# Scatters of rows that no longer wait for one another, in a fused attention and mixture-of-experts kernel

## The chip, the cores and the metric

The kernel runs on one core of a Trainium2 chip. The metric is the device time of one execution in microseconds (us). The kernel before takes 4299.98 us, the median of three runs (4298.31 to 4304.7).

## The reference

Three stages run on 24576 tokens (8 batches of 3072) of width 256, all in float32.

```python
# 1 attention without softmax, gated by u
attn = np.maximum(z @ z.T / S, 0.0) ** 2          # per batch, S = 3072, z is S x 64
x = u * (attn @ v)
# 2 dense layer, d_ff = 1024
h = x @ w_in;  e = np.exp(h - h.max(-1)); solu = h * e / (e.sum(-1) + 1e-9)
x = (solu - mean) / np.sqrt(var + 1e-6) * g_ln @ w_out
# 3 one expert of eight per token
logits = x @ w_gate;  expert = argmax(logits);  gate = softmax(logits)[expert]
out[mask_e] = gate[mask_e] * (np.maximum(x[mask_e] @ w1[e], 0) @ w2[e])
```

## The kernel before, in words

Products are made at nearly float32 accuracy by splitting each operand into a high and a low part and adding three matmuls (`mm3`, lines 104 to 107).

**The main stage** walks through 48 chunks of 512 tokens. A chunk takes 24 slots, one slot for each block of 128 keys; there are 1152 slots (NS). A dictionary `events` lists what else is done in a slot: loads, and, for the chunk before, the dense layer (`blk_h` to `blk_y`) and the routing (`blk_scale`, `blk_logits`, `blk_route`, `blk_rows`). The program is written out in the order of slots, and each engine does its own instructions strictly in that order. The routing passes small tiles between GpSimd and VectorE: GpSimd computes `vv` (lines 600 to 604), VectorE needs it at line 608, and so on at lines 642 and 648 and at lines 676 and 679.

**The scatter of rows.** When the expert and the place of each token are known, `blk_scatter` (lines 684 to 691) writes 128 rows of 264 floats to a table in HBM, `sorted_rows`, by an indirect DMA that GpSimd issues. There are four per chunk, 192 in all. Rows of one expert lie together, so the table can then be read in units of one expert each.

**The expert stage** has 62 units: 37 of 512 rows whose places are fixed by an early table (made after 44 chunks are counted, by `table_step(0, ...)`), 4 of 512 rows and 21 of 256 rows from a later table. Each has 8 steps. In step k, `up(k)` makes one eighth of the hidden layer, and `downs` multiplies the eighth of two steps before (LAG = 2) by w2. Around the steps of a unit stand the loads of a later unit: its rows by `load_x` (line 843; issued by GpSimd for units 0 and 1, by SyncE for the rest), its weights by `load_w` (line 849), split into high and low parts by ScalarE and VectorE at lines 854 and 855. The last chunks' dense layer and routing run between the first steps of this stage, on the same engines.

**The scatter of outputs.** After the last step of a unit, `down` copies one or two PSUM banks of 128 x 512 to SBUF (line 926 on VectorE, line 928 on ScalarE, in turn) and right behind each copy writes two indirect DMAs to the output (line 931). There are 206 of them, all issued by GpSimd. Each row of the output is written once.

**What orders these DMAs.** Dependencies are worked out tile by tile from what an instruction reads and writes. All scatters of rows write the same table, and an indirect write may touch any row of it. So each scatter of rows waits until the scatter before it has landed, and until loads of unit rows that were issued before it have landed; and each load of unit rows waits for all scatters before it. Scatters of outputs wait for one another likewise. The wait stands on the issuing engine's queue (GpSimd, or SyncE for loads), and what is written behind it on that engine waits too.

In one slot the order is: scores, buffers taken, `up(k)`, the events of the slot, the attention products, `downs(k - LAG)`, then the elementwise work.

Of the kernel before, what the change touches and what calls it, by code (L numbers as in the profile page):

```python
# [10 lines left out]
F32 = mybir.dt.float32  # L11
# [3 lines left out]
U32 = mybir.dt.uint32  # L15
# [18 lines left out]
def attention_moe_kernel(ctx, tc, u, v, z, w_in, w_out, g_ln, w_gate, w1, w2, out):  # L34
    nc = tc.nc
    B, S, D = u.shape
# [4 lines left out]
    N = B * S  # L41
# [29 lines left out]
    n_early = max(0, -(-(SNAP * CH - NE * (FULL - 1)) // FULL))  # L71
    n_late = max(0, -(-(N - n_early * FULL - NE * (FULL - 1)) // FULL))
    n_half = (N - (n_early + n_late) * FULL + NE * (HALF - 1)) // HALF
    units = [FULL] * (n_early + n_late) + [HALF] * n_half
    NU = len(units)
# [4 lines left out]
    const = ctx.enter_context(tc.tile_pool(name="const", bufs=1))  # L80
# [13 lines left out]
    tail_i = const.tile([1, NE], I32, name="tail_i")  # L94
    n_used = const.tile([1, NE + 1], F32, name="n_used")
    index = const.tile([1, n_most], F32, name="index")

    V, A, G, T = nc.vector, nc.scalar, nc.gpsimd, nc.tensor

# [29 lines left out]
    with ExitStack() as st:  # L129
# [4 lines left out]
        ap = st.enter_context(tc.tile_pool(name="ap", bufs=2))  # L134
# [363 lines left out]


        h_t, p_t, pt_t, y_t, st_t = {}, {}, {}, {}, {}  # L500
        pb_t, pT_t = {}, {}

        def blk_h(c, t, kd):
# [88 lines left out]
        def small(name, shape, dt=F32):  # L592
            return sp.tile(shape, dt, tag=name, name=name)
# [41 lines left out]
        def blk_route(c, part):  # L635
            s, y = st_t[c], y_t[c]
            k4 = 4 * NE
            if part == 0:
                s["m"] = small("gm", [P, 4])
                V.tensor_reduce(out=s["m"], in_=s["lg"], axis=AX.X, op=ALU.max)  # L640
            elif part == 1:
                G.tensor_tensor(out=s["lg"], in0=s["lg"], in1=s["m"].unsqueeze(2).to_broadcast([P, 4, NE]),
                                op=ALU.subtract)
            elif part == 2:
                s["ex"] = small("gx", [P, 4, NE])
                A.activation(out=s["ex"], in_=s["lg"], func=AF.Exp)
                s["key"] = small("gk", [P, 4, NE])
                V.scalar_tensor_tensor(out=s["key"], in0=s["lg"], scalar=0.0, in1=first_key,
                                       op0=ALU.is_equal, op1=ALU.mult)
            elif part == 3:  # L650
                V.tensor_reduce(out=s["m"], in_=s["key"], axis=AX.X, op=ALU.max)
                s["gs"] = small("gs", [P, 4])
                V.tensor_reduce(out=s["gs"], in_=s["ex"], axis=AX.X, op=ALU.add)
            elif part == 4:
                s["oh"] = small("oh", [P, 4, NE], BF16)
                V.tensor_tensor(out=s["oh"], in0=s["key"], in1=s["m"].unsqueeze(2).to_broadcast([P, 4, NE]),
                                op=ALU.is_equal)
                G.tensor_scalar(out=s["gs"], in0=s["gs"], scalar1=1e-9, scalar2=0.0, op0=ALU.add, op1=ALU.add)
            elif part == 5:
                oh = s["oh"]  # L660
                s["cum"] = cum = small("cum", [P, 4, NE], BF16)
                G.tensor_copy(out=cum[:, 0], in_=counts)
                for t in range(3):
                    G.tensor_tensor(out=cum[:, t + 1], in0=cum[:, t], in1=oh[:, t], op=ALU.add)
                G.tensor_tensor(out=counts, in0=cum[:, 3], in1=oh[:, 3], op=ALU.add)
                V.reciprocal(out=s["gs"], in_=s["gs"])
                G.tensor_scalar(out=y[:, :, D], in0=row_id, scalar1=float(c * CH), scalar2=0.0,
                                op0=ALU.add, op1=ALU.add)
            elif part == 6:
                s["rk"] = rk = ps_m.tile([P, CH], F32, tag="m", name="rk")  # L670
                T.matmul(out=rk[:, :k4], lhsT=upper, rhs=s["oh"].rearrange("p t e -> p (t e)"), start=True, stop=False)
                T.matmul(out=rk[:, :k4], lhsT=ones, rhs=s["cum"].rearrange("p t e -> p (t e)"), start=False, stop=True)
                s["ps"] = small("ps", [P, 4, NE])
                V.tensor_tensor(out=s["ps"], in0=rk[:, :k4].rearrange("p (t e) -> p t e", t=4), in1=e_base, op=ALU.add)
            elif part == 7:
                G.tensor_tensor(out=s["ps"], in0=s["ps"], in1=s["oh"], op=ALU.mult)
            elif part == 8:
                s["pf"] = small("pf", [P, 4])
                V.tensor_reduce(out=s["pf"], in_=s["ps"], axis=AX.X, op=ALU.add)
            else:  # L680
                s["pi"] = small("pi", [P, 4], I32)
                G.tensor_copy(out=s["pi"], in_=s["pf"])

        def blk_scatter(c, t):
            pi = st_t[c]["pi"]
            G.indirect_dma_start(  # L686
                out=xs[:DUMMY], out_offset=bass.IndirectOffsetOnAxis(ap=pi[:, t:t + 1].bitcast(U32), axis=0),
                in_=y_t[c][:, t, :], in_offset=None, bounds_check=DUMMY - 1, oob_is_err=False)
            if t == 3:
                y_t.pop(c)  # L690
                st_t.pop(c)
# [69 lines left out]
                    V.tensor_tensor(out=n_used[:, :NE], in0=n_used[:, :NE], in1=now, op=ALU.add)  # L761
                yield

        table = {}

        def table_step(key, *args):
            if key not in table:
                table[key] = unit_table(*args)
            next(table[key], None)

        def pad_tail(e):
# [8 lines left out]
        raw_w, w_set, xT_t, hT_b, o_b, xr_t, gi_t, id_t = {}, {}, {}, [], [], {}, {}, {}  # L780
# [45 lines left out]
        def dma_of(i):  # L826

            return G if i < 2 else nc.sync

        def load_x(i, part=None):  # L830

            n = units[i]
            if not part:
                x_row[i] = dma_of(i).value_load(row_i[0:1, i:i + 1], min_val=0, max_val=DUMMY - (n if n == FULL else 0))
                xr_t[i] = xrow.tile([P, KD * CH], F32, tag="x", name="x")
                gi_t[i] = sp.tile([P, FULL // P], F32, tag="gi", name="gi", bufs=6)
            xv = xr_t[i][:, :KD * n].rearrange("p (k a j) -> p k a j", k=KD, j=32)
            unit = xs[ds(x_row[i], n)]
            src = unit[:, :D].rearrange("(a i) (k b j) -> k b i a j", i=32, b=4, j=32)
            todo = [(xv[b * 32:(b + 1) * 32, k], src[k, b]) for b in range(4) for k in range(KD)]  # L840
            todo.append((gi_t[i][:, :n // P], unit[:, D:D + 1].rearrange("(q p) w -> p (q w)", p=P)))
            for dst, x in todo if part is None else todo[3 * part:3 * part + 3]:
                dma_of(i).dma_start(out=dst, in_=x)

        def load_w(i, k):
            e = dma_of(i).value_load(expert_i[0:1, i:i + 1], min_val=0, max_val=NE - 1)
# [30 lines left out]
        LAG = 2  # L877
# [3 lines left out]
        def piece(i, name, at, n):  # L881
            return w_set[i % 2, name][at // CH][:, at % CH:at % CH + n]
# [27 lines left out]
        def down(k):  # L910
            i, m = steps[k]
            hT = hT_t.pop(k)
            if m == 0:
                y_p[i] = y_banks(i)
            for r in range(units[i] // P):
                rs = slice(r * P, (r + 1) * P)
                y = y_p[i][r // 2][:, r % 2 * D:(r % 2 + 1) * D]
                mm3(y, hT[0][:, rs], hT[1][:, rs], piece(i, "w2h", m * D, D), piece(i, "w2l", m * D, D),
                    m == 0 and r % 2 == 0, m == KE - 1, skip_group_check=True)
            if m < KE - 1:  # L920
                return
            for h, y in enumerate(y_p.pop(i)):
                o_n[0] += 1
                o = o_b[o_n[0] % len(o_b)]
                if o_n[0] % 2:
                    V.tensor_copy(out=o, in_=y)
                else:
                    A.activation(out=o, in_=y, func=AF.Copy)
                for r in range(2):
                    q = 2 * h + r  # L930
                    G.indirect_dma_start(
                        out=out, out_offset=bass.IndirectOffsetOnAxis(ap=id_t[i][:, q:q + 1].bitcast(U32), axis=0),
                        in_=o[:, r * D:(r + 1) * D], in_offset=None, bounds_check=N - 1, oob_is_err=False)

        def downs(k):

# [6 lines left out]
        for c in range(NCHUNK):  # L943
# [11 lines left out]
            else:  # L955

                late = j >= NCB - 2
# [59 lines left out]
        early = [(0, n_early, FULL)], False  # L1017
        late = [(n_early, n_late, FULL), (n_early + n_late, n_half, HALF)], True
# [26 lines left out]
        for part in range(3):  # L1045
            at(s0 + XA + 3 * part, load_x, 0, part)
# [11 lines left out]
        for i in range(NU):  # L1058
            k0 = NS + i * KE
            k1 = k0 + KE  # L1060
            late = max(0, 5 - i)
# [16 lines left out]
        with tc.manual_schedule():  # L1078
            for n in range(min(lo_slot, -LA), hi_slot + 1):
                i = n + LA  # L1080
                k = n - NS
                if 0 <= i < NS and not is_kept(i):
                    pe_scores(i)
                for fn, args in events.get(n, []):
                    if fn is take:
                        fn(*args)
                if 0 <= k < NP:
                    up(k)
                for fn, args in events.pop(n, []):
# [52 lines left out]
```

## Time and profile before

| | us |
|---|---|
| median of 3 runs | 4299.98 |
| the profiled execution's own time | 4297.59 |
| its span, first to last instruction | 4296.0 |
| TensorE busy (98% of the span) | 4218.8 |
| VectorE busy (74%) | 3173.4 |
| ScalarE busy (65%) | 2773.7 |
| GpSimd busy (32%) | 1368.9 |

Mean granted TensorE clock: 0.994 of full speed. The 16 DMA engines moved 719.11 MB.

In the profile PE is TensorE's matmuls, PEld its weight loads, DVE VectorE, ACT ScalarE, POOL GpSimd, SP SyncE; a q behind a name is the engine's sequencer. `out_y L931` and the like name the tile written and the line of the kernel. An arrow in brackets names the instruction that ended an idle time; a DMA there means that its data had landed. PEclk is the mean clock granted to TensorE in a stretch: 1.00 is 2.4 GHz, 0.50 is 1.2 GHz, and values between mean that it changed within the stretch.

### The profile page before, as it was taken

The numbers are of one execution on the slowest core, as the hardware profiler recorded it, in microseconds if no ns is written. First come the engines' busy times: TensorE is split into PE (matmuls) and PEld (weight loads), VectorE is DVE, ScalarE is ACT, GpSimd is POOL, SyncE is SP. The second block draws the span as 40 slices with busy tenths as digits, with TensorE's granted clock in tenths as the row PEclk, the third lists the DMA queues.
The fourth block names the chain that finished last, engine by engine and source line by source line (L and its number), as shares of the span: only waits on it lengthen the run. The fifth ranks groups of instructions, "written<-read, shape, count | busy, mean of one in ns | idle before, by whom it ended". The sixth has DMA issues, their size and how long they took to land.

```text
span 4296.0 us, 74103 instructions
## 1 busy us (share of the span) xinstructions
PE 4218.8 (98%) x23314; PEld 3659.4 (85%) x23314; DVE 3173.4 (74%) x5485; ACT 2773.7 (65%) x5104; POOL 1368.9 (32%) x2852
## 2 busy tenths in 40 slices
PE   7999999999999999999999999999889999999998
PEld 5888888888888888888888888888788899999998
DVE  8778787777878777787877778777655555555686
ACT  7767776776777677667767766775544444444565
POOL 5135224323522432352244235224322111111111
PEclk9999999999999999999999999999999999999999
DMA  6898789789888988997898898789655555555585
GB/s 160 168 173 180 171 181 176 165 183 174 179 170 182 175 166 183 173 177 171 182 174 168 183 174 176 169 169 181 143 143 132 147 147 134 145 137 147 156 221 162
DMA packets 2444332, 719.11 MB, mean 167 GB/s; under 512 B 2251933, under 2 KB 2325917, under 8 KB 2443936
## 3 DMA queue, kind: packets, MB, share of 16 engines
q1 hardware_dynamic: 2402016, 603.29, 69.2%
q0 software_dynamic: 40864, 110.95, 8.7%
q8 instruction: 182, 2.98, 0.3%
q14 instruction: 214, 1.75, 0.1%
q10 hardware_dynamic: 1056, 0.13, 0.0%
HBM read 442.35 MB, written 273.49 MB: 167 GB/s over the span
## 4 chain that ended last, share of the span: by engine, by line
PE 81%; issue 5%; DMA 4%; DVE 2%; SPq 2%; POOL 1%; ACT 1%; POOLq 0%; DVEq 0%; ACTq 0%
PE o L105 11%; PE o L106 11%; PE o L107 11%; PE yp L105 4%; PE yp L107 4%; PE yp L106 4%; PE h L512 4%; PE h L513 4%; PE h L516 4%; PE s L444 3%; PE s L445 3%; PE y L107 3%; PE y L106 3%; PE y L105 3%; PE g L105 3%
## 5 line engine op out<-in xcount | busy, mean ns | idle before, releaser
L106 PE MATMUL o<-al,vw 128*128 128x512 f32 x2304 | 908.2, 394 | 7.8 <-DVE al L465 7.3
L105 PE MATMUL o<-ah,vw 128*128 128x512 f32 x2304 | 907.8, 394 | 1.7 <-DVE ut L489 1.7
L107 PE MATMUL o<-ah,vw 128*128 128x512 f32 x2304 | 898.7, 390 | 0.0
L450 ACT ACTIVATE r<-s 128x512 f32<-128x512 f32 x704 | 416.7, 592 | 405.6 <-PE s L445 397.1
L460 ACT ACTIVATE ah<-a 128x512 fp32r<-128x512 f32 x832 | 525.3, 631 | 201.6 <-issue 99.5
L465 DVE TENSOR_TENSOR al<-a,ah 128x512 fp32r<-128x512 f32 x832 | 581.4, 699 | 15.7 <-ACT ah L460 14.7
L107 PEld LDWEIGHTS o<-ah,vw 128*128 128x128 f32 x2304 | 433.7, 188 | 94.4
L106 PEld LDWEIGHTS o<-al,vw 128*128 128x128 f32 x2304 | 433.6, 188 | 94.2 <-DVE al L465 16.3
L105 PEld LDWEIGHTS o<-ah,vw 128*128 128x128 f32 x2304 | 433.6, 188 | 84.9 <-ACT ah L460 2.1
L455 ACT ACTIVATE a<-r 128x512 f32<-128x512 f32 x704 | 438.0, 622 | 58.2 <-DVE al L465 29.5
L899 ACT ACTIVATE zw_x<-g 128x512 fp32r<-128x512 f32 (+1 forms) x332 | 179.9, 542 | 428.9 <-PE g L107 425.2
L107 PE MATMUL yp<-gw,ptl 128*128 128x264 f32 x1536 | 437.8, 285 | 7.0 <-DVE ptl L102 7.0
L105 PE MATMUL yp<-gw,pth 128*128 128x264 f32 x1536 | 438.8, 286 | 1.1 <-ACT pth L101 1.1
L106 PE MATMUL yp<-gw,pth 128*128 128x264 f32 x1536 | 438.0, 285 | 0.0
L900 DVE SCALAR_TENSOR_TENSOR zw_x<-g,zw_x 128x512 fp32r<-128x512 f32 (+1 forms) x332 | 205.6, 619 | 308.8 <-ACT zw_x L899 308.7
L102 DVE TENSOR_TENSOR ptl<-pT,pth 128x512 fp32r<-128x512 f32 x384 | 264.2, 688 | 215.8 <-ACT pth L101 213.7
L686 POOL DMA_INDIRECT sorted_rows<-y,pi x192 | 211.7, 1102 | 390.3 <-DMA sorted_rows<-y,pi 307.9
L513 PE MATMUL h<-w_in,xt 128*128 128x512 f32 x768 | 304.9, 397 | 0.0
L512 PE MATMUL h<-w_in,xt 128*128 128x512 f32 x768 | 304.6, 397 | 0.0
L105 PEld LDWEIGHTS yp<-gw,pth 128*128 128x128 f32 x1536 | 289.2, 188 | 16.9 <-ACT pth L101 1.5
L106 PEld LDWEIGHTS yp<-gw,pth 128*128 128x128 f32 x1536 | 289.9, 189 | 15.0
L107 PEld LDWEIGHTS yp<-gw,ptl 128*128 128x128 f32 x1536 | 290.1, 189 | 7.7 <-DVE ptl L102 7.7
(271 smaller groups left out, 10665.7 us busy)
## 6 DMA issues: line engine op xcount, KB each, us to landing
vw_x<-in_moe_w SPq DMA_DIRECT2D x120, 1024.0 KB
pT<-moved SPq DMA_DIRECT2D x768, 128.0 KB
sym<-kept SPq DMA_DIRECT2D x1520, 64.0 KB
kept<-sym SPq DMA_DIRECT2D x316, 256.0 KB
moved<-pb SPq DMA_DIRECT2D x528, 128.0 KB
moved<-pb POOLq DMA_DIRECT2D x240, 128.0 KB, 3.1
x<-sorted_rows SPq DMA_DIRECT2D x312, 64.0 KB
sym<-kept SPq DMA_DIRECT2D x68, 256.0 KB
```

The costliest lines, as they stand in the source:

```text
L102: V.tensor_tensor(out=lo, in0=src, in1=hi.bitcast(F32), op=ALU.subtract)
L105: T.matmul(out=out, lhsT=lh, rhs=rh, start=start, stop=False, **kw)
L106: T.matmul(out=out, lhsT=lh, rhs=rl, start=False, stop=False, **kw)
L107: T.matmul(out=out, lhsT=ll, rhs=rh, start=False, stop=stop, **kw)
L450: A.activation(out=r, in_=s_t.pop(n), func=AF.Relu)
L455: A.activation(out=a, in_=r_t.pop(n), func=AF.Square)
L460: A.activation(out=h, in_=a_t[n], func=AF.Copy)
L465: V.tensor_tensor(out=l, in0=a_t[n], in1=ah_t[n].bitcast(F32), op=ALU.subtract)
L512: T.matmul(out=h[:, fs], lhsT=w[:, 0, kd, ts_], rhs=w_in_t[0][:, kd, fs], start=(kd == 0), stop=False)
L513: T.matmul(out=h[:, fs], lhsT=w[:, 0, kd, ts_], rhs=w_in_t[1][:, kd, fs], start=False, stop=False)
L686: G.indirect_dma_start(out=xs[:DUMMY], out_offset=bass.IndirectOffsetOnAxis(ap=pi[:, t:t + 1].bitcast(U32), axis=0), in_=y_t[c][:, t, :], ...
L900: V.scalar_tensor_tensor(out=lo, in0=h, scalar=0.0, in1=hi.bitcast(F32), op0=ALU.max, op1=ALU.subtract)
```

## The change

Four things are changed.

- A scatter of rows is declared independent of other scatters of rows and of the loads of the 37 early units. The loads of the early units are declared independent of scatters of chunks that the early table did not count ("late rows"). They still wait for scatters of counted chunks, and loads of later units still wait for all.
- Scatters of outputs are declared independent of one another.
- A scatter of outputs is not written behind its eviction any more, but at the start of a later step: one step later for the first bank of a unit, two steps later for the second. Those of the last unit stay where they were.
- Ahead of every scatter, and ahead of a group of row loads that GpSimd issues, GpSimd clears one float (`between`).

```diff
+        def between():
+            G.memset(gap, 0.0)
+
+        def apart(i, *groups, why):
+            for g in groups:
+                tc.declare_no_dep(i.ins, group=g, reason=why)
+
         def blk_scatter(c, t):
             pi = st_t[c]["pi"]
-            G.indirect_dma_start(
+            between()
+            i = G.indirect_dma_start(
                 out=xs[:DUMMY], out_offset=bass.IndirectOffsetOnAxis(ap=pi[:, t:t + 1].bitcast(U32), axis=0),
                 in_=y_t[c][:, t, :], in_offset=None, bounds_check=DUMMY - 1, oob_is_err=False)
+            apart(i, "rows", "late rows", why="every token has a row of its own")
+            apart(i, "early units", why="units of the early table are full of rows counted before")
+            tc.add_to_no_dep_group("late rows" if table and c not in counted else "rows", i.ins)
...
+            if dma_of(i) is G:
+                between()
             for dst, x in todo if part is None else todo[3 * part:3 * part + 3]:
-                dma_of(i).dma_start(out=dst, in_=x)
+                d = dma_of(i).dma_start(out=dst, in_=x)
+                if i < n_early:
+                    apart(d, "late rows", why="units of the early table are full of rows counted before")
+                    tc.add_to_no_dep_group("early units", d.ins)
...
                 for r in range(2):
-                    q = 2 * h + r
-                    G.indirect_dma_start(
-                        out=out, out_offset=bass.IndirectOffsetOnAxis(ap=id_t[i][:, q:q + 1].bitcast(U32), axis=0),
-                        in_=o[:, r * D:(r + 1) * D], in_offset=None, bounds_check=N - 1, oob_is_err=False)
+                    if i == NU - 1:
+                        send(i, 2 * h + r, o[:, r * D:(r + 1) * D])
+                    else:
+                        sends[k + 1 + h].append((i, 2 * h + r, o[:, r * D:(r + 1) * D]))
+
+        sends = defaultdict(list)
+
+        def send(i, q, o):
+            between()
+            d = G.indirect_dma_start(
+                out=out, out_offset=bass.IndirectOffsetOnAxis(ap=id_t[i][:, q:q + 1].bitcast(U32), axis=0),
+                in_=o, in_offset=None, bounds_check=N - 1, oob_is_err=False)
+            apart(d, "out", why="every token has a row of its own")
+            tc.add_to_no_dep_group("out", d.ins)
...
                     if fn is take:
                         fn(*args)
+                for args in sends.pop(k - LAG, []):
+                    send(*args)
                 if 0 <= k < NP:
                     up(k)
```

(`counted` holds the chunks whose routing was written before the early table is begun.)

## Rows read from the trace of the kernel before

**Rows 1.** Busy us, instructions, PEclk, DMA share and GB/s by stretch:

```profile
200.00:3000.00 2800.00, 2795.94 (x14227) 2370.94 (x14227) 2206.66 (x3779) 1995.57 (x3598) 1034.55 (x2422) 1.00 0.88 175
3000.00:3420.00 420.00, 386.57 (x2326) 345.33 (x2325) 247.16 (x461) 185.14 (x342) 111.60 (x192) 0.96 0.57 139
3420.00:4283.00 863.00, 862.71 (x5981) 806.13 (x5980) 558.21 (x995) 446.37 (x898) 154.30 (x155) 1.00 0.60 159
```

**Rows 2.** Waits of PE from 3000 to 3420: us in total, times, longest:

```profile
PE g L105 <- DVE zw_x L900: 26.3, 7, 7.1
PE yp L107 <- DVE ptl L102: 6.6, 1, 6.6
```

**Rows 3.** Timeline of PE: start, us, instruction, idle before it and its releaser:

```profile
3050.45 0.50 PE L105 MATMUL g<-vw_x 128*128 128x512 f32 x1 [0.99 <-DVE zw_x L900]
...
3359.16 0.79 PE L105 MATMUL g<-a_x,zd_x 128*128 128x512 f32 x1 [3.40 <-DVE zw_x L900]
...
3387.00 0.80 PE L105 MATMUL g<-vw_x 128*128 128x512 f32 x1 [3.57 <-DVE zw_x L900]
```

**Rows 4.** Stretches of 10 us from where PE resumes (columns of rows 1):

```profile
3016.53:3026.53 10.00, 10.00 (x45) 8.79 (x46) 6.59 (x10) 3.54 (x6) 5.95 (x19) 0.78 0.64 132
3103.01:3113.01 10.00, 10.00 (x59) 9.17 (x60) 8.66 (x16) 3.64 (x7) 5.30 (x17) 0.83 0.21 55
3137.35:3147.35 10.00, 10.00 (x54) 8.96 (x55) 8.71 (x18) 4.76 (x9) 3.26 (x10) 0.84 0.21 52
3171.27:3181.27 10.00, 10.00 (x54) 8.94 (x55) 8.96 (x15) 4.76 (x9) 3.62 (x3) 0.83 0.30 87
3230.12:3240.12 10.00, 10.00 (x44) 8.85 (x45) 4.39 (x8) 1.72 (x3) 1.94 (x8) 0.70 0.81 158
3359.16:3369.16 10.00, 10.00 (x54) 8.92 (x55) 9.64 (x33) 4.51 (x9) 2.97 (x3) 0.84 0.17 61
3387.00:3397.00 10.00, 10.00 (x48) 8.73 (x49) 8.00 (x28) 4.39 (x9) 1.94 (x2) 0.70 0.67 214
```

**Rows 5.** Waits of DVE for POOL from 3000 to 3420:

```profile
DVE yi L608 <- POOL vv L604: 24.6, 3, 9.1
...
DVE gk L648 <- POOL lg L642: 12.5, 1, 12.5
...
DVE pf L679 <- POOL ps L676: 9.2, 1, 9.2
```

**Rows 6.** Timeline of POOL around the stall that ends at 3137.35:

```profile
3118.94 1.07 POOL L931 DMA_INDIRECT out_y<-a_x,ids  x1 [9.21 <-DVE a_x L926]
...
3132.89 0.98 POOL L931 DMA_INDIRECT out_y<-a_x,ids  x1 [3.22 <-DMA out_y<-a_x,ids]
3133.88 0.26 POOL L642 TENSOR_TENSOR lg<-lg,gm 128x32 f32<-128x32 f32 x1
```

**Rows 7.** Timeline of POOL before the stall that ends at 3016.53:

```profile
3013.06 1.02 POOL L686 DMA_INDIRECT sorted_rows<-y,pi  x1 [4.64 <-DMA gi<-sorted_rows]
```

**Rows 8.** Waits of SP's queue, 3150 to 3420, and ACT's timeline at 3357:

```profile
SPq L843 <- DMA sorted_rows<-y,pi: 43.6, 4, 17.5
...
3357.15 0.63 ACT L854 ACTIVATE vw_x<-vw_x 128x512 fp32r<-128x512 f32 x1 [6.41 <-DMA vw_x<-in_moe_w]
```

**Rows 9.** Timeline of POOL, the last two scatters:

```profile
4284.25 0.97 POOL L931 DMA_INDIRECT out_y<-p_x,ids  x1 [6.84 <-DVE p_x L926]
4286.60 0.97 POOL L931 DMA_INDIRECT out_y<-p_x,ids  x1 [1.39 <-DMA out_y<-p_x,ids]
```

**Rows 10.** Line 931: ns min/median/max of scatters from `a_x`, and all landings:

```profile
L931 POOL DMA_INDIRECT out_y<-a_x,ids x108: 967/972/1608, 3087.2 to 4267.4; - x108
...
DMA to landing us min/median/max: 2.1/3.6/6.8
```

**Rows 11.** POOL's smallest clear (groups by line: busy us, mean ns of one):

```profile
L1127 POOL MEMSET const-float32-1.0<- 128x1 f32 x1 | 0.1, 99 | 0.0
```

**Rows 12.** Waits of ACT from 300 to 2950:

```profile
ACT pth L101 <- DMA pT<-moved: 30.2, 21, 4.7
```

More of the change, by code (lines that the diff above doesn't have):

```diff
@@ L96, in attention_moe_kernel @@
     index = const.tile([1, n_most], F32, name="index")
+    gap = const.tile([1, 1], F32, name="gap")
     V, A, G, T = nc.vector, nc.scalar, nc.gpsimd, nc.tensor
@@ L500, in attention_moe_kernel @@
         h_t, p_t, pt_t, y_t, st_t = {}, {}, {}, {}, {}
+        table, routed, counted = {}, [], []
         pb_t, pT_t = {}, {}
@@ L665, in blk_route @@
                 G.tensor_tensor(out=counts, in0=cum[:, 3], in1=oh[:, 3], op=ALU.add)
+                routed.append(c)
                 V.reciprocal(out=s["gs"], in_=s["gs"])
@@ L762, in unit_table @@
                 yield
-        table = {}
         def table_step(key, *args):
@@ L768, in table_step @@
                 table[key] = unit_table(*args)
+                if key == 0:
+                    counted.extend(routed)
             next(table[key], None)
```

## The prediction

> **What bounds the kernel now.** I read the busy time by stretch first, to see where TensorE (PE) is not full [rows 1]. From 200 to 3000 us it is idle for 4.06 of 2800 us, and from 3420 to 4283 for 0.29 of 863: there PE is the bound, and shorter waits on GpSimd (POOL) or SyncE (SP) buy nothing. Between them, from 3000 to 3420, it is idle for 33.4 of 420 us and its clock averages 0.96. This is where the last chunks' routing runs among the first expert units, and the only place where the change can pay much. The long waits of POOL elsewhere are no loss; a reader who adds them up over the span would expect far too much.
>
> Then PE's waits in that stretch: 6.6 us once and 26.3 us in seven pieces, all ended by VectorE (DVE) [rows 2]. In PE's timeline one of the seven is a mere 0.99 us at 3050 [rows 3]; without it seven stalls are left, together 6.6 + 26.3 - 0.99 = 31.9 us. Behind each of them the clock is low: in the 10 us after PE resumes it averages 0.70 to 0.84, so part of that time ran at 1.2 GHz and the rest at 2.4 [rows 4]. The work lost there is 10 us times one minus the clock: 2.2 + 1.7 + 1.6 + 1.7 + 3.0 + 1.6 + 3.0 = 14.8 us. The stage is full and at full speed elsewhere, so the seven stalls cost 46.7 us with their slow restarts.
>
> Last, who was late. Five stalls are DVE waiting for a small routing result of POOL: 24.6 us in three waits, 12.5 in one and 9.2 in one, 46.3 in sum [rows 5]. POOL's own timeline says why: for the stall that ends at 3137, POOL began the four scatters of a unit at 3118.94, each held until the one before had landed, and got to the routing at 3133.88, 14.9 us later, though the instruction itself takes 0.26 us [rows 6]. For the stall that ends at 3016 the scatters of rows did the same and also waited for loads of unit 0, up to 4.64 us at a time [rows 7]. DVE works in order, so the split of the next hidden layer stood behind the routing instruction that waited, and PE behind that. The other two stalls, 3.40 and 3.57 us [rows 3], come from SP: loads of unit rows waited 43.6 us in four pieces, the longest 17.5, for scatters of rows of the last chunks; the weight loads queue behind them, and ScalarE (ACT) then sat 6.41 us waiting for weights [rows 8].
>
> **The change part by part.**
>
> *Waits between scatters go.* POOL is held by a scatter only for its own instruction, 0.97 us at the median and 1.61 at most [rows 10], and the added clear, for which 0.1 us is taken from POOL's smallest one [rows 11]. Four scatters in a row so cost 4 x 1.07 = 4.3 us, at worst 4 x 1.71 = 6.8, in place of 14.9. Even if all four stood ahead of the routing, as now, the result at 3133.88 would come 8.1 to 10.6 us sooner, more than the 7.1 us that PE stalled [rows 2]. The same test for the five together: their 46.3 us of DVE waits turned into 31.9 - 3.40 - 3.57 = 24.9 us of PE stalls, so PE stands about (46.3 - 24.9) / 5 = 4.3 us of such a wait without loss. The five waits average 9.3 us. If each shrinks by the share of [rows 6], 10.6 of 14.9, 2.7 us are left of it, and by the worst share, 8.1 of 14.9, 4.2 us: both within the margin, the second barely. All five are counted as gone.
>
> *Scatters of outputs move one and two steps back.* At most two then stand in one step, ahead of that step's `up` and routing on POOL, and their data were evicted one step before, so POOL no longer sits at their head for the eviction with routing behind. What moves is 204 of 206 indirect DMAs, on POOL's queue alone; SP's and ACT's order is untouched. The SBUF buffers of the evictions stay occupied 1 to 2 steps longer, but are used again only after one unit of 8 steps (two buffers, at the start) or two (four buffers). A landing takes 6.8 us at most [rows 10], while the 8 steps of a unit of 256 rows are about 12 us long and of one of 512 rows about 22. Cost: nothing; this cover would be gone only if a scatter took a whole unit.
>
> *Loads of early units no longer wait for late rows.* The four waits, 43.6 us, leave SP's queue. In the two that hurt, the weight loads come forward by up to 17.5 us, where PE needed 3.4 and 3.6. What is next on SP is the wait for a free weight buffer, which paces these loads in the units without a stall. Counted as gone.
>
> *The clears.* One per scatter and per group of loads on POOL, some 400 x 0.1 = 40 us over the run, on an engine that works 1034.55 of 2800 us in its busiest stretch [rows 1]. Cost on the path: nothing but the tail.
>
> *The tail.* The last scatter starts 1.39 us after the one before it ended, waiting for its landing [rows 9]. That goes, a clear and a short issue gap come: about 1.0 us gained, 0 to 1.3 as bounds.
>
> *The main stage.* Its 176 scatters sit two slots apart in program order. PE has 4.06 us to give back there in all; I take 0 of it.
>
> **The sum.** 31.9 + 14.8 + 1.0 = 47.7 us. Against the profiled execution's own time, 4297.59 (span 4296.0 and 1.6 around it), that is 4249.9. This execution was 2.4 us below the median of the runs, so the forecast of the median is 4299.98 - 47.7 = 4252.3, say 4252. What is late after it: nothing with a stall of over 1 us before 4283; PE's share of the span rises above 98%.
>
> **The rivals.**
>
> *A. A new wait takes the place of part of it.* With POOL out of the way the weights are next: ACT already waits for them at the two SP stalls, and when PE runs 35 us earlier the 1 MB loads have less time. If the two weight stalls stay, their 3.40 + 3.57 us and the clock behind them (1.6 + 3.0 in rows 4) remain, 11.6 us: 4264. Twice as many give 4276. Against it: these loads are paced by buffers that DVE frees, so they move forward with PE.
>
> *B. Nothing moves.* If the declared independence left the waits in place, or if scatters in a row held POOL as long as now, the stalls stay: about 4299. This needs 12 us for four scatters, 3 us each; none of the 108 in the row took over 1.61 [rows 10]. The Trainium skill has a rule for this case: by SBUF — State Buffer, section Who interferes with whom, DVE in a two-port mode locks POOL out of the port that they share, and the same page tells of a POOL-issued DMA that took about 3100 ns beside a DVE copy instead of 620. By that rule four scatters beside evictions would hold POOL 12.4 us and the gain would be near zero. This trace speaks against it: the evictions on DVE already run next to these scatters, and the row's maximum is half of that.
>
> *C. Slower: the scatters crowd the main stage's DMAs.* There the DMA share is 0.88 at 175 GB/s [rows 1]. A scatter moves 128 x 264 x 4 B = 135 KB, 0.77 us of all the DMA engines at that rate; four together could put off the loads that attention and the dense layer wait for by 3.1 us. If the middle of 0 and 3.1, 1.55 us, reached PE in each of 45 chunks, 70 us would come on top: 4322. It decides from 47.7 / 45 = 1.06 us per chunk. For it: ACT already waits for such a load up to 4.7 us [rows 12]. Against it: those waits, 30.2 us in 21 pieces, all lie inside 4.06 us of PE idle, and the scatters stay two slots apart. The skill's rule in DMA: Bandwidth & Descriptors, section Queues, rings and completion order, speaks for crowding: each DMA engine takes turns between the queues that have work, packet by packet, so a burst from POOL would share with SP's loads. No run so far shows such a burst.
>
> **How the numbers follow.** The forecast has 0.72, A 0.16 (two thirds of it at 4264, the rest up to 4280), B 0.06, C 0.06. The forecast's own range is 4243 (the 4.06 us of the main stage, the 0.99 and some 4 us of spread in the runs on top) to 4258. The range that leaves out about one in ten on the side of B and C takes in A: 4243 to 4280. A measurement can tell 0.2%, 8.6 us, from no change: faster means below 4291.4. The forecast and A are faster, 0.88; B is the same, 0.06; C slower, 0.06.
>
> **What would show it right or wrong.** Right: from 3000 us to where the stretch ends, PE idle falls from 33 us to under 3 and the clock stays at 1.00; DVE's waits on POOL at lines 608, 648 and 679 fall below 4 us each; POOL's scatters show no landing of another scatter as releaser; SP's line 843 no longer waits for scatters of rows in early units; from 200 to 3000 PE idle stays at about 4 us. If POOL's waits are gone but PE still idles with a weight DMA behind ACT, A holds. If scatters still wait, or last 3 us, B does. If idle time appears in the main stage with a load of `pT` or `sym` ahead of it, C does. The forecast is wrong as a whole if the stalls go and the time does not, that is, if PE then stalls later for something that these stalls covered.

## The result, and the profile after

The changed kernel takes 4248.33 us, the median of four runs (4246.93 to 4251.76), against 4302.31 for the kernel before in four runs (4298.31 to 4304.7; one run more than stood ahead of the prediction). The ratio is 0.9877, with a 95% interval of 0.9863 to 0.9892. The profiled execution took 4248.69 us (span 4247.1), 48.9 us less than the one before.

The busy time by stretch of the changed kernel, in the columns of [rows 1]:

```profile
200.00:3000.00 2800.00, 2797.58 (x14246) 2373.96 (x14246) 2203.90 (x3781) 1991.91 (x3598) 1073.57 (x2610) 1.00 0.83 175
3000.00:3420.00 420.00, 418.12 (x2623) 376.10 (x2622) 276.17 (x507) 207.16 (x383) 125.71 (x272) 1.00 0.63 156
3420.00:4234.00 814.00, 813.06 (x5657) 760.26 (x5656) 529.52 (x947) 422.81 (x857) 163.84 (x288) 1.00 0.60 159
```

In the stretch of the seven stalls PE is now idle for 1.88 us in place of 33.4, and the clock is 1.00. The waits of PE from 2990 to 3420, against [rows 2]; the one wait of 1.0 us is the piece that the prediction had set aside in [rows 3]:

```profile
PE g L106 <- DVE zw_x L919: 1.0, 1, 1.0
PE g L107 <- DVE vw_x L103: 0.4, 1, 0.4
PE o L107 <- DVE al L466: 0.4, 1, 0.4
PE yp L108 <- DVE ptl L103: 0.2, 1, 0.2
```

POOL's timeline at the place of [rows 6], now with the clears (L688):

```profile
3101.41 1.06 POOL L958 DMA_INDIRECT out_y<-a_x,ids  x1 [10.19 <-DVE a_x L945]
3102.48 0.09 POOL L688 MEMSET gap<- 1x1 f32 x1
3102.78 1.00 POOL L958 DMA_INDIRECT out_y<-a_x,ids  x1 [0.21 <-issue]
3103.79 0.26 POOL L644 TENSOR_TENSOR lg<-lg,gm 128x32 f32<-128x32 f32 x1
3103.97 0.09 POOL L688 MEMSET gap<- 1x1 f32 x1
3104.25 0.99 POOL L958 DMA_INDIRECT out_y<-a_x,ids  x1 [0.18 <-issue]
...
3105.54 0.98 POOL L958 DMA_INDIRECT out_y<-a_x,ids  x1 [0.22 <-issue]
```

The routing instruction comes 2.4 us after the first scatter began, not 14.9: the first pair takes 2.4 us with its clear and a gap of 0.2, and the second pair stands behind the routing. No scatter names a landing any more. The waits of VectorE in this stretch name no routing result of POOL any more (46.3 us before, [rows 5]). POOL itself still stands at the head of the scatters until VectorE has made the copy out of PSUM (10.19 us in the first row). VectorE's row for that copy:

```profile
3100.44 0.68 DVE L945 COPY a_x<-y 128x512 f32<-128x512 f32 x1
```

The scatter instruction itself did not get dearer by following another at once, against [rows 10] (ns min/median/max):

```profile
L958 POOL DMA_INDIRECT out_y<-a_x,ids x108: 971/976/1502, 3075.1 to 4218.0; - x108
```

On SP's queue, 3150 to 3420, the unit rows no longer wait for scatters; what waits for one (5.0 us, line 788) is the padding of the table, as it must ([rows 8] had 43.6 us):

```profile
SPq L788 <- DMA sorted_rows<-pad_row: 14.2, 4, 4.6
SPq L788 <- DMA sorted_rows<-y,pi: 5.0, 1, 5.0
```

The last two scatters, against [rows 9]: about 0.3 us lie between them in place of 1.39, a clear among them.

```profile
4236.42 0.97 POOL L958 DMA_INDIRECT out_y<-p_x,ids  x1 [7.84 <-DVE p_x L945]
4237.38 0.09 POOL L688 MEMSET gap<- 1x1 f32 x1
4237.70 0.97 POOL L958 DMA_INDIRECT out_y<-p_x,ids  x1 [0.23 <-issue]
```

So the time came from the stretch that the prediction named. Which part of the change gave it is another question, and there the experiments surprised.

### The profile page after: what moved, and what is told of

Read it like the earlier page. It is cut to its first block, busy times and chain, and to the rows that moved or that the text cites. A ratio compares the mean times of both kernels' runs of the same rounds, so it can differ in the third digit from the quotient of the medians.

```text
span 4247.1 us, 74510 instructions
## 1 busy us (share of the span) xinstructions
PE 4203.5 (99%) x23314; PEld 3648.4 (86%) x23314; DVE 3171.4 (75%) x5485; ACT 2768.4 (65%) x5104; POOL 1431.7 (34%) x3254
## 4 chain that ended last, share of the span: by engine, by line
PE 93%; issue 1%; DVE 1%; DMA 1%; POOL 0%; ACT 0%; SPq 0%; DVEq 0%; POOLq 0%; ACTq 0%
PE o L106 12%; PE o L107 12%; PE o L108 12%; PE yp L106 4%; PE yp L108 4%; PE yp L107 4%; PE y L108 4%; PE y L107 4%; PE y L106 4%; PE h L514 4%; PE h L515 4%; PE h L518 4%; PE g L106 4%; PE g L107 4%; PE g L108 4%; PE s L445 3%
## 5 line engine op out<-in xcount | busy, mean ns | idle before, releaser
L466 DVE TENSOR_TENSOR al<-a,ah 128x512 fp32r<-128x512 f32 x832 | 579.1, 697 | 15.6 <-ACT ah L461 14.7
L107 PEld LDWEIGHTS yp<-gw,pth 128*128 128x128 f32 x1536 | 289.4, 188 | 14.9
L530 DVE TENSOR_REDUCE nm<-h 128x1 f32<-128x1024 f32 x192 | 234.6, 1222 | 87.0 <-PE h L518 68.3
L445 PE MATMUL s<-zw 128*128 128x512 f32 x704 | 277.2, 394 | 16.2 <-ACT r L451 9.2
```

The source lines that it names most:

```text
L107: T.matmul(out=out, lhsT=lh, rhs=rl, start=False, stop=False, **kw)
L445: T.matmul(out=s, lhsT=w, rhs=z_t[c], start=True, stop=False)
L466: V.tensor_tensor(out=l, in0=a_t[n], in1=ah_t[n].bitcast(F32), op=ALU.subtract)
L530: V.tensor_reduce(out=s["nm"][:, t:t + 1], in_=h, axis=AX.X, op=ALU.max, negate=True)
```

## The experiments

The theory: POOL, held by landings of scatters, made five of the stalls, and the loads of unit rows that wait for late scatters made the other two. The main rival inside it: the place of the output scatters in POOL's order matters, not only their waits. Gains below are differences of medians within one set of runs, where the kernel before had 4304.0, 4301.9 and 4302.2 us. Each diff is against the changed kernel, so its minus lines are parts of the change that the run leaves out; `...` stands for cut code. The clears stay in every run, so no run shows what they do by themselves.

**One part alone.** Outputs only:

```diff
-            apart(i, "rows", "late rows", why="every token has a row of its own")
-            apart(i, "early units", ...)
-            tc.add_to_no_dep_group("late rows" if table and c not in counted else "rows", i.ins)
...
-                if i < n_early:
-                    apart(d, "late rows", ...)
-                    tc.add_to_no_dep_group("early units", d.ins)
...
-                        sends[k + 1 + h].append((i, 2 * h + r, o[:, r * D:(r + 1) * D]))
+                        send(i, 2 * h + r, o[:, r * D:(r + 1) * D])
```

> Only the scatters of outputs are made independent; they stay right behind their evictions, and scatters of rows and loads of units wait as before. Theory (POOL was held by landings): four of the seven stalls, 4.2 + 7.1 + 3.8 + 3.3 = 18.4 us, go with the 8.0 us of slow clock behind them, and about 1 us at the tail: 27 us less than the kernel before. Of the stall near 3010 us and of the two that the loads of unit rows cause, 20 us with their clock, most stays. Rival (the place of the scatters in POOL's order matters: POOL stands at the head of the four for the eviction): those four stalls only shrink, 5 to 15 us less.

Measured: 4256.46 us, 47.6 less than before (ratio 0.9891, 0.9876 to 0.9906). Both were wrong, far too low. Its waits of PE from 2985 to 3420:

```profile
PE yp L108 <- DVE ptl L103: 3.8, 1, 3.8
PE y L106 <- DVE p_x L939: 1.2, 1, 1.2
```

The four stalls behind output scatters are gone, as the theory had it. But of the two on weights only 0.2 us and 1.2 are left too, as waits for evictions that VectorE makes behind the split of the weights, though the loads still wait 34.5 us for scatters of rows. The stall near 3010 is left, with 3.8 us in place of 6.6. No output scatter has been issued by then, so that difference is not theirs: the first scatter of rows ahead of it waited 1.2 us for a load to land in place of 4.6, here and in the next run. Whether that comes from the clears or from the execution stays open.

Move only, that is the kernel before with the move and the clears, and with all waits in place:

```diff
-            apart(d, "out", why="every token has a row of its own")
-            tc.add_to_no_dep_group("out", d.ins)
```

(and without the edits to `blk_scatter` and `load_x` as in the run above).

> Only the scatters of outputs are moved one and two steps back; all of them, scatters of rows and loads wait for one another as before. Theory: POOL is still held for every landing, about 3 us each, but at most two in one step, so routing that stands between the pairs comes about half as late; the four stalls shrink by something between a fifth and all of their 26 us with clock: 5 to 25 us less than before, 13 as the middle. Rival (only the waits for landings matter, not the place): no change, within 3 us.

Measured: 4262.04 us, 42.0 less (0.9905, 0.9890 to 0.9920). The place in the order alone gives most of the gain; the rival is out and the theory's range was too low. PE's waits of over 1 us are 5.5 and 4.3 us, two stalls in place of seven. POOL at the one near 3098:

```profile
3081.32 0.97 POOL L952 DMA_INDIRECT out_y<-a_x,ids  x1 [11.02 <-DVE a_x L939]
...
3095.01 0.97 POOL L952 DMA_INDIRECT out_y<-a_x,ids  x1 [2.12 <-DMA out_y<-a_x,ids]
3096.05 0.23 POOL L602 TENSOR_SCALAR vv<-se 128x4 f32<-128x4 f32 x1
```

Here all four scatters are still ahead of the routing, and it comes 14.7 us after the first began. At the next place the routing stands between the pairs, and VectorE waits 4.7 us in place of 12.5.

Rows only, with output scatters as before:

```diff
-            apart(d, "out", why="every token has a row of its own")
-            tc.add_to_no_dep_group("out", d.ins)
...
-                        sends[k + 1 + h].append((i, 2 * h + r, o[:, r * D:(r + 1) * D]))
+                        send(i, 2 * h + r, o[:, r * D:(r + 1) * D])
```

> Only the scatters of rows and the loads of early units are made independent; scatters of outputs wait and stand as before. Theory: the stall near 3010 us (6.6 us and 2.2 of clock) and the two near 3356 and 3384 us (7.0 and 4.6) go: 20 us less than before; the four stalls behind scatters of outputs, 26 us with clock, stay. Rival (the two late stalls are the scatters of outputs, which hold the last scatters of rows back): only 9 us less.

Measured: 4275.55 us, 28.5 less (0.9932, 0.9919 to 0.9946). Exactly the three stalls that the theory named are gone, and the rival is out; four are left, 3.83, 6.78, 2.94 and 3.26 us, the same four as before. The profiled executions differ by 23.6, the medians by 28.5.

Loads only, a smaller edit still: as the run above, and

```diff
-            apart(i, "rows", "late rows", why="every token has a row of its own")
-            apart(i, "early units", why="units of the early table are full of rows counted before")
```

> The kernel before with one edge taken away: loads of early units do not wait for scatters of late rows. All scatters wait for one another, scatters of rows wait for loads, nothing is moved. Theory (the two late stalls need both: loads that wait, and a scatter of rows that stands late behind the landings of scatters of outputs; so either alone cures them): the stalls at 3356 and 3384 us go with their clock, 12 us less than before; the five stalls behind POOL stay, the one near 3010 us perhaps 4 us shorter because loads of unit 0 no longer wait for a scatter. Rival (the waits of loads are not what made the weights late): both late stalls stay, within 3 us of before.

Measured: 4274.70 us, 27.5 less (0.9936, 0.9922 to 0.9949), no different from rows only. The two stalls on weights are gone, and so is the one near 3010, which was expected to shrink by 4 us: VectorE's wait there is 1.27 us, and PE does not feel that (the table under "A dose of lateness" shows how much it bears). The rival is out. Four stalls are left: 4.65, 5.60, 2.93 and 4.14 us.

**One part taken away again.** The whole change without the move:

```diff
-                    if i == NU - 1:
-                        send(i, 2 * h + r, o[:, r * D:(r + 1) * D])
-                    else:
-                        sends[k + 1 + h].append((i, 2 * h + r, o[:, r * D:(r + 1) * D]))
+                    send(i, 2 * h + r, o[:, r * D:(r + 1) * D])
```

> The whole change but for the move: scatters of outputs are independent and stand right behind their evictions. Theory (the waits were the matter, not the place): as the changed kernel, about 53 us less than before, within 4 us of it; POOL's four scatters in a row take 4.3 us, within the margin of about 4.3 us that PE has. Rival (the place matters): at least one of the four stalls comes back, 10 us or more slower than the changed kernel.

Measured: 4248.08 us, 56.0 less (0.9870, 0.9855 to 0.9885): the changed kernel's time. Once no scatter waits for a landing, its place does not matter; four in a row make VectorE wait 2.5 us at most, and no stall of PE comes from that.

The whole change without the freedom of the loads:

```diff
-                    apart(d, "late rows", why="units of the early table are full of rows counted before")
```

> The changed kernel, but loads of early units wait again for scatters of chunks that the early table did not count. Theory: the two late stalls on weights come back, 7.0 us and 4.6 of clock, so 12 us more than the changed kernel (about 41 us less than before). Rival (those stalls came from scatters held up behind scatters of outputs, which no longer happens): within 2 us of the changed kernel.

Measured: 4248.71 us, 53.2 less (0.9876, 0.9860 to 0.9893). The theory fell: the loads wait 29.7 us for scatters, and no stall comes back. The weights' issue on SP shows why. In each fence the first row is the last pair of weight loads ahead of the late unit rows and the second the pair behind them. The fences are from the kernel before, outputs only, and this run:

```profile
3312.75 9.33 SPq L849 DMA_DIRECT2D vw_x<-in_moe_w  x2
...
3352.03 1.61 SPq L849 DMA_DIRECT2D vw_x<-in_moe_w  x2
```

```profile
3280.91 9.33 SPq L862 DMA_DIRECT2D vw_x<-in_moe_w  x2
...
3316.77 1.61 SPq L862 DMA_DIRECT2D vw_x<-in_moe_w  x2
```

```profile
3277.35 9.32 SPq L867 DMA_DIRECT2D vw_x<-in_moe_w  x2
...
3310.08 1.61 SPq L867 DMA_DIRECT2D vw_x<-in_moe_w  x2
```

The pairs lie 39.3, 35.9 and 32.7 us apart; in the changed kernel the same two lie 22.5 apart (3274.64 and 3297.09). So the weights were 16.8, 13.4 and 10.2 us later than there, and PE stalled for 3.40, about 0.2 and 0 us. Some 13 us of lateness are free here, and only what lies beyond reached PE. In this run the loads' wait for scatters stays below that. In the kernel before it went above, where the scatter of rows came 9.8 us after the first of four output scatters that each waited for a landing; with outputs only it came 5.6 us after it.

The smallest edit, without the move and without the freedom of the loads: the whole change with the last two diffs together.

> The changed kernel without the move and without the freedom of the loads: scatters of outputs and of rows are independent, scatters of rows do not wait for loads of early units, loads wait for all scatters. Theory (the waits of POOL were the whole cause): as the changed kernel, within 4 us. Rival (with neither the move nor the free loads the weights are late again): stalls near 3330 and 3350 us, 5 to 12 us more than the changed kernel.

Measured: 4250.48 us, 51.7 less (0.9882, 0.9867 to 0.9897), within the interval of the changed kernel. Near 3343 us PE waits 1.2 us for an eviction that VectorE makes behind the split of the weights; that is all that is left of the rival. The same two pairs of weight loads lie 35.5 us apart (3274.75 and 3310.27), 13.0 us late, so this edit stands at the edge of what is free.

**A dose of lateness.** Clears ahead of line 602 in the last three chunks, 24 and 60:

```diff
+                for _ in range(60 if c >= NCHUNK - 3 else 0):
+                    G.memset(gap, 0.0)
                 s["vv"] = vv = small("vv", [P, 4])
```

> The changed kernel with 24 more clears of one float on POOL ahead of line 602 in each of the last three chunks, some 4 us of POOL's time each. Theory (DVE waits for POOL's routing, PE stands 4.3 us of that): DVE waits up to 4 us at three places, PE stalls little: 0 to 4 us more than the changed kernel. Rival (no margin): 12 us and their clock, about 18 us more. Rival (POOL's lateness was not the cause): nothing at all, and no wait of DVE at this place.

> As the run with 24, with 60 clears, some 10 to 11 us of POOL's time at each of three places. Theory: DVE waits 7 to 10 us there, PE stalls for what goes beyond 4.3 us, 3 to 6 us each, and runs at the low clock afterwards, 1.6 to 3 us lost each: 14 to 27 us more than the changed kernel. Rival (POOL's lateness was not the cause): no change.

Measured: 4249.70 us with 24 (ratio 0.9879, 0.9863 to 0.9896), no change, and 4262.55 with 60 (0.9912, 0.9896 to 0.9929), some 14 more than the changed kernel, at the theory's lower end. With 24, VectorE waited at most 3.4 us for this routing step, and PE lost nothing to it. With 60, VectorE's waits at the three places and PE's three stalls:

```profile
3008.21 0.17 DVE L612 TENSOR_SCALAR yi<-vv 128x4 int32<-128x4 int32 x1 [4.44 <-POOL gap L690]
...
3093.26 0.17 DVE L612 TENSOR_SCALAR yi<-vv 128x4 int32<-128x4 int32 x1 [8.54 <-POOL vv L608]
...
3204.99 0.17 DVE L612 TENSOR_SCALAR yi<-vv 128x4 int32<-128x4 int32 x1 [6.11 <-POOL gap L690]
```

```profile
3009.16 0.39 PE L108 MATMUL yp<-gw,ptl 128*128 128x264 f32 x1 [3.08 <-DVE ptl L103]
...
3094.09 0.80 PE L106 MATMUL g<-a_x,ur_x 128*128 128x512 f32 x1 [3.65 <-DVE zw_x L921]
...
3206.42 0.50 PE L106 MATMUL g<-a_x,ur_x 128*128 128x512 f32 x1 [1.82 <-DVE zw_x L921]
```

The kernel before has the same pairs at five places, VectorE's wait first and then PE's stall:

```profile
3015.58 0.17 DVE L608 TENSOR_SCALAR yi<-vv 128x4 int32<-128x4 int32 x1 [7.94 <-POOL vv L604]
...
3102.18 0.17 DVE L608 TENSOR_SCALAR yi<-vv 128x4 int32<-128x4 int32 x1 [9.06 <-POOL vv L604]
...
3134.17 0.19 DVE L648 SCALAR_TENSOR_TENSOR gk<-lg,first_key 128x32 f32<-128x32 f32 x1 [12.47 <-POOL lg L642]
...
3168.10 0.19 DVE L679 TENSOR_REDUCE pf<-ps 128x4 f32<-128x32 f32 x1 [9.16 <-POOL ps L676]
...
3228.70 0.17 DVE L608 TENSOR_SCALAR yi<-vv 128x4 int32<-128x4 int32 x1 [7.60 <-POOL vv L604]
```

```profile
3016.53 0.59 PE L107 MATMUL yp<-gw,ptl 128*128 128x264 f32 x1 [6.58 <-DVE ptl L102]
...
3103.01 0.80 PE L105 MATMUL g<-a_x,ur_x 128*128 128x512 f32 x1 [4.18 <-DVE zw_x L900]
...
3137.35 0.80 PE L105 MATMUL g<-vw_x 128*128 128x512 f32 x1 [7.09 <-DVE zw_x L900]
...
3171.27 0.80 PE L105 MATMUL g<-a_x,ur_x 128*128 128x512 f32 x1 [3.77 <-DVE zw_x L900]
...
3230.12 0.79 PE L105 MATMUL g<-a_x,ur_x 128*128 128x512 f32 x1 [3.31 <-DVE zw_x L900]
```

Set beside the other runs, each wait less its stall is the same at one place, whatever made POOL late (us; wait, then stall):

| start of the stall in the kernel before, result waited for | kernel before | other runs | wait less stall |
|---|---|---|---|
| 3010, `vv` | 7.94, 6.58 | outputs only 5.13, 3.76; move only 5.65, 4.28; 60 clears 4.44, 3.08 | 1.4 |
| 3099, `vv` | 9.06, 4.18 | move only 10.42, 5.54; rows only 8.71, 3.83; loads only 9.53, 4.65; 60 clears 8.54, 3.65 | 4.9 |
| 3130, `lg` | 12.47, 7.09 | rows only 12.16, 6.78; loads only 10.98, 5.60 | 5.4 |
| 3168, `ps` | 9.16, 3.77 | rows only 8.33, 2.94; loads only 8.32, 2.93 | 5.4 |
| 3227, `vv` | 7.60, 3.31 | rows only 7.55, 3.26; loads only 8.43, 4.14; 60 clears 6.11, 1.82 | 4.3 |

So each place bears its own share of lateness, 1.4 to 5.4 us, and what goes beyond reaches PE in full. The prediction's 4.3 us is the mean of the five.

**Crowding.** All four scatters of a chunk in one slot:

```diff
-                at(e + more * (18 + t * (1 if NCHUNK - 4 < c and not last else 2)), blk_scatter, c, t)
+                at(e + more * 18 if c < NCHUNK - 4 else e + more * (18 + t * (...)), blk_scatter, c, t)
```

(`(...)` stands for the expression of the line above it.)

> The changed kernel, but in all chunks up to the 44th the four scatters of rows stand in one slot, not two slots apart. Theory: they reach the DMA queues within some 5 us, about 3 us of all the DMA engines' time at 175 GB/s, and the loads of the main stage have that much margin: no change, within 3 us of the changed kernel. Rival (crowding): up to 1.5 us per chunk reach PE, up to 66 us more.

Measured: 4247.19 us (0.9874, 0.9857 to 0.9890), no change. The four start within 4 us of one another (1426.57 to 1430.54 in one chunk), and PE's idle time from 200 to 2980 does not grow. Crowding is out.

## Why the prediction was right, and where its parts were not

The forecast was 4252, the measurement 4248.33, within the range. By the terms of the sum, in the profiled pair: the seven stalls and the slow clock behind them went as a whole (46.7 us), the tail gave 1.1 (from the start of PE's last matmul to the end of the span 13.0 us before and 12.0 after) for the forecast's 1.0, and the main stage 1.6 (idle 4.06 to 2.42) where 0 was taken. That makes 49.4; from 3420 us on PE idles for 0.94 us in place of 0.29, which leaves 48.7 against the 48.9 measured. The 1.6 us of the main stage do not come from the waits between scatters of rows: outputs only and move only show 2.3 us of idle time there too, though POOL still waits over 250 us for landings of scatters in either. The clears are in all these runs and not in the kernel before, of which there is one trace, so whether the 1.6 us are theirs stays open. The medians differ by 54.0. The profiled execution of the kernel before was among its fastest (it ran from 4297.7 to 4307.4 in the first set of experiments); where its slower executions lost some 5 us more stays open.

*Waits between scatters go*: right. The pair cost 2.4 us, the dispatch stayed at 0.98 us at the median and 1.5 at most. Its margin of 4.3 us was a mean and not a bound: had the 4.2 us of its worst case been left near 3010 us, where PE bears 1.4, a stall of some 2.8 us would have stayed. In the changed kernel no wait is listed there at all, which the test on the mean could not tell. The rule on the shared port that the prediction cites from the Trainium skill (SBUF — State Buffer, section Who interferes with whom) did not show: the longest output scatter after the change is half of the 3.1 us that the same page tells of. The rule is for VectorE in a two-port mode; no run here shows that the evictions, which read PSUM, use one.

*Scatters of outputs move back*, costed at nothing: right for the kernel as it is, since without the move the time is the same. But its reason fell. POOL was to sit no longer at the head of the scatters for the eviction; in the stretch from 3000 to 3420 it does so for 211.5 us in 15 waits with the move and for 213.0 in 15 without. In the timeline of the profile after, the scatter at 3101.41 starts 0.3 us after its copy out of PSUM ends, and the routing instruction stands behind the pair. The prediction also missed that the move together with the clears would pay 42 us with all waits in place. It can put half of the scatters behind the routing, and that suffices where it brings VectorE's wait under what the place bears: in move only `lg` comes 4.7 us late and `ps` 2.6, where 5.4 is free, and PE does not stall.

*Loads of early units no longer wait*: here the prediction's cause was incomplete. It put the two stalls on weights, 11.6 us with their clock, down to the loads' wait. That wait is needed for them but not enough: put back, it costs nothing (loads wait again); taken away alone, it cures both of them and also the one near 3010 (loads only). The prediction had put that third stall under the waits of scatters. It was both: scatters of rows and loads of unit 0 waited for one another in turn on POOL.

The parts therefore don't add up: outputs only, move only and rows only gave 47.6, 42.0 and 28.5 us, 118 in sum, and together 54. Five of the seven stalls have more than one cure: the two on weights go with any of the three parts, and three of those behind output scatters go with their independence or with their move. The prediction was spared by summing over the stalls, not over the edits.

Rival A did not come: no stall on weights is left. B is out, as no scatter waits for a landing any more; C is out by the run with the scatters in one slot.

## What to carry to other kernels

Read the gain from the stalls of the engine that bounds the kernel, with the slow clock behind each, and not from the waits that a change removes: POOL waited some 290 us for landings of scatters in the main stage, and with these waits gone PE's idle time there is 2.4 us, as it is where they stay (2.3 us in outputs only). Ask of each late engine how late it may be for free, place by place and not on the mean, since a half cure that brings it under that margin is worth as much as a whole one. And where a stall has two waits in series, do not price the edits one by one: undo each from the finished kernel and add each to the old one, for only the two together tell whether it is needed.

## What the runs showed of the hardware

Stalls of near equal length did not all cost a slow clock. In the 10 us after the stalls of 3.08, 3.65 and 1.82 us in the run with 60 clears, the granted clock (the number after POOL's) was 1.00, 0.72 and 1.00: 2.4 GHz throughout, 1.2 GHz for part of the time, and 2.4 GHz throughout.

```profile
3009.16:3019.16 10.00, 10.00 (x54) 8.67 (x55) 8.62 (x13) 4.55 (x8) 7.29 (x21) 1.00 0.59 129
3094.09:3104.09 10.00, 10.00 (x50) 9.16 (x51) 7.95 (x15) 2.61 (x4) 5.33 (x18) 0.72 0.21 55
3206.42:3216.42 10.00, 10.00 (x61) 8.97 (x62) 6.41 (x12) 3.84 (x7) 3.28 (x12) 1.00 0.81 182
```

After two stalls at the same place, 2.94 us in rows only and 2.93 in loads only, it was 0.83 and 1.00. In the kernel before PE ran at 1.2 GHz for part of the 10 us after each of the seven stalls, the shortest of which was 3.31 us ([rows 4]).
